# A list schedule of its own for an attention and gated-MLP kernel, and float16 halves for the row of reciprocals

## The chip, the core and the metric

The kernel runs on one NeuronCore of a Trainium2 chip. The core has five engines with one instruction queue each: TensorE (PE: matrix products, with weight loads shown apart as PEld), VectorE (DVE), ScalarE (ACT), GpSimd (POOL) and SyncE (SP, which here only issues DMAs). Each queue is worked off in its order; engines wait for each other by semaphores. The metric is the device time of one execution in microseconds (us), lower is better.

## The reference

Attention over 8 batches, 12 heads, 448 positions, 64 columns, with an RMS norm on queries and keys, and then a gated MLP that mixes positions:

```python
q_n, k_n = (rmsnorm(q, g_q), rmsnorm(k, g_k))          # x / sqrt(mean(x*x) + 1e-6) * g
scores = scale * np.matmul(q_n, k_n.transpose(0, 1, 3, 2))
scores = scores - np.max(scores, axis=-1, keepdims=True)
attn = np.exp(scores)
attn = attn / (np.sum(attn, axis=-1, keepdims=True) + 1e-09)
x = np.matmul(attn, v)                                  # heads side by side: (8, 448, 768)
h = gelu_tanh(x @ w_in)                                 # 768 -> 1024
u, v = h[..., :512], h[..., 512:]
v_n = (v - mean(v)) / np.sqrt(var(v) + 1e-6) * g_ln
v_s = np.einsum('ts,bsd->btd', w_sg, v_n) + b_sg[None, :, None]
out = x + (u * v_s) @ w_out                             # 512 -> 768
```

Everything is float32. The kernel keeps that precision with pairs of float16 numbers: a value is split into a high half and the rest, and a product is made of three (high x high, high x low, low x high).

## The kernel before, in words

The work goes by *head pairs*: two heads of one batch, 48 pairs in all, index `i`; two pairs with the same loads form a unit `u` (24 of them), six pairs a batch `b`.

- For a unit, `load_qk` brings queries and keys; `squares` and `norms` make the reciprocal norms (ScalarE squares, VectorE sums, L311, L312); `split` multiplies them in on GpSimd (L336, L337), makes the float16 halves (L341 ScalarE, L342 GpSimd) and transposes them by DMA into `qt`.
- `scores(u)` has seven tiles `t`. For each tile six (or twelve half-height) matmuls write two banks (L418), VectorE takes the maximum (`nm`, L421), ScalarE the exponential with its sum (`ex`, L424), ScalarE the high half and VectorE the rest (`ahl`, L427, L428), and SyncE issues the transpose into `at_all` (L433). After tiles 3 and 6 `recips` takes the reciprocals of the sums (L385, L386).
- `pv(i)` first spreads the reciprocals over a row by matmuls against an identity (`recip_row`, L398: eight float32 matmuls, four blocks by two heads; ScalarE copies the row, L401), then makes 3 + 18 matmuls of values and attention (L450, L455), multiplies by the row (L457) and splits the result into the halves of `x` (L459, L460).
- `moe(b)` is the MLP of a batch: `mv` (L517, L520: the half of `w_in` that makes `v`), a cluster of Gelu activations between two table loads (`cluster`, L470 to L479), the layer norm, `mu` (L576), Gelu again, `ms` (L604, L611: the mixing of positions), the gating on GpSimd (L615 to L619), `mo` (L642 to L654: `w_out` and the residual).
- `weights()` decodes `w_in`, `w_sg` and `w_out` once, in the first batch (L150 to L156, L197 to L199, L230 to L256).

TensorE's matmuls come in several *tile forms*: 128*128 (the whole array), 64*128 for scores (two row halves), 128*64 for pv, rows and a part of mv (two column halves), 64*64.

PSUM: two score tiles of two banks (`ps_s`), one bank for rows and pv (`ps_v`), three for all of the MLP (`ps_m`).

What sets the order before: the program is written as generators (`scores`, `pv`, `moe`, `weights`) that the loop at the end advances in turn, by ratios (`SC`, `SV`, `M0`, `M1`, `MR`, `ML`, `WR`), with priorities shifted for the MLP (`MOFF`, `GP`). The tile framework's own scheduler, with its timeline simulation (`TILE_KW`), makes the queues from that. The MLP of batch `b` runs beside the attention of the next batch; those of the first and the last batch use another form of `moe` (`early=True`), in which two mv tiles take each pair's `x` as it comes.

Of the kernel before, what the change touches and what calls it, by code (L numbers as in the profile page):

```python
# [23 lines left out]

MOFF, MOFF0, GP = 200, 100, 350

WR, M0, M1, MR, ML = 3, 8, 7, 11, 11

SLOT = (0, 4, 1, 5, 2, 6, 3)

I0, WD = 5, 6

VC, UC = (3,), (0, 1)

SC, SV = 7, 3
# [5 lines left out]
EXP_SET = "natural_log_exp_and_others"  # L41
BACC_KW = dict(dynamic_dma_scratch_size=1024)
TILE_KW = dict(schedule_with_timeline_sim=True)
# [3 lines left out]
def kernel(  # L47
# [14 lines left out]
    nc = tc.nc  # L62
# [18 lines left out]
    FH = DH // 2  # L81

    const = ctx.enter_context(tc.tile_pool(name="const", bufs=1))
    ld = ctx.enter_context(tc.tile_pool(name="ld", bufs=3))
    prep = ctx.enter_context(tc.tile_pool(name="prep", bufs=2))
    att = ctx.enter_context(tc.tile_pool(name="att", bufs=2))
    sml = ctx.enter_context(tc.tile_pool(name="sml", bufs=4))
    xp = ctx.enter_context(tc.tile_pool(name="xp", bufs=1))
    ps_s = ctx.enter_context(tc.tile_pool(name="ps_s", bufs=NS, space=bass.MemoryType.PSUM))
    ps_v = ctx.enter_context(tc.tile_pool(name="ps_v", bufs=NV, space=bass.MemoryType.PSUM))  # L90
    ps_m = ctx.enter_context(tc.tile_pool(name="ps_m", bufs=NM, space=bass.MemoryType.PSUM))
    mlp = None

    V, A, G = nc.vector, nc.scalar, nc.gpsimd
    mm = nc.tensor.matmul
# [3 lines left out]
    G.memset(ones, 1.0)  # L99
    ident = const.tile([P, P], BF16, name="ident")  # L100
    make_identity(nc, ident)
    ident_f = const.tile([P, P], F32, name="ident_f")
    V.tensor_copy(out=ident_f, in_=ident)
    warm = sml.tile([P, 1], F32, name="warm", bufs=1)
    A.preload_act_table_set(EXP_SET)
    A.activation(out=warm, in_=ones[:, 0:1], func=AF.Square)

    SSW = 2 * C7
# [34 lines left out]

    W = {}

    def decode(dst, raw, tmp):
# [6 lines left out]
        hf = raw.bitcast(F32)[:, :, 1]  # L153
        A.activation(out=tmp, in_=hf, func=AF.Square)
        G.tensor_scalar(out=tmp, in0=tmp, scalar1=LEAST_SQ, scalar2=None, op0=ALU.is_ge)
        G.tensor_tensor(out=dst, in0=dst, in1=tmp, op=ALU.mult)  # L156

    def weights():
        nonlocal mlp
        ctx_w = ExitStack()  # L160

        wi = const.tile([P, KT, 2, DF], F16, name="wi")
        wi_f = wi.rearrange("p t x f -> p t (x f)").bitcast(F32)
        ws_h = const.tile([P, CK, S], F16, name="ws_h")
        ws_l = const.tile([P, CK, S], F16, name="ws_l")
        wo_h = const.tile([P, FT, DM], F32R, name="wo_h")
        wo_l = const.tile([P, FT, DM], F32R, name="wo_l")
        gw = const.tile([P, FT], F32, name="gw")
        bb = const.tile([P, S], F32, name="bb")
        part = const.tile([P, 2 * KT], F32, name="wi_part")  # L170
        stage = ctx_w.enter_context(tc.tile_pool(name="stage", bufs=1))
        WC = DF // 2
        raws = {}

        def load_raw(j):
            if j >= 2 * KT:
                return
            raws[j] = stage.tile([P, WC, 2], I32, name="raw", bufs=RAWB)
            nc.sync.dma_start(out=raws[j].rearrange("p a b -> p (a b)"),
                         in_=wi_b[j // 2 * P:(j // 2 + 1) * P, (j % 2) * 2 * WC:(j % 2 + 1) * 2 * WC])  # L180

        with tc.issue_after(first):
            for j in range(RAWB):
                load_raw(j)
        for j in range(2 * KT):
            dst = wi_f[:, j // 2, (j % 2) * WC:(j % 2 + 1) * WC]
            sq = prep.tile([P, 896], F32, name="sqk", tag="t4", bufs=HLB)
            decode(dst, raws.pop(j), sq[:, 0:WC])
            load_raw(j + RAWB)
            sq2 = stage.tile([P, WC], F32, name="sqw", bufs=2)  # L190
            A.activation(out=sq2, in_=dst, func=AF.Square, accum_out=part[:, j:j + 1])
            yield
        wsc, winv = pow2_scale("wi", part, const)
        W["winv"] = winv
        for t in range(KT):
            tmp = stage.tile([P, DF], F32, name="tmp", bufs=2)
# [3 lines left out]
            yield  # L200
        W.update(wi_h=wi[:, :, 0], wi_l=wi[:, :, 1])
        ctx_w.close()

        mlp = ctx.enter_context(tc.tile_pool(name="mlp", bufs=1))
        W.update(ws_h=ws_h, ws_l=ws_l, wo_h=wo_h, wo_l=wo_l, gw=gw, bb=bb)
        yield

        wsr = [mlp.tile([P, S], F32, name="wsr", tag="ug", bufs=5) for c in range(CK)]  # L210
        for s_ in range(C7):
            nc.sync.dma_start(out=wsr[s_ // 2][s_ % 2 * HP:(s_ % 2 + 1) * HP],
                              in_=w_sg.rearrange("(p c) s -> c p s", c=C7)[SLOT[s_]])
# [7 lines left out]
        yield  # L221
        for c in range(CK):
            np_ = P if c < CM else HP
# [3 lines left out]
            for o, n, src in ((0, C4, cols[:, 0:C4]), (HP, CM, cols[:, C4:C7]), (S, 1, cols[:, CM:C4])):  # L227
                oh, ol = (x[0:np_, o - o % P:o - o % P + n * P].rearrange("t (c p) -> t c p", p=P)[:, :, o % P:o % P + HP]
                          if n > 1 else x[0:np_, o:o + HP].unsqueeze(1) for x in (wph, wpl))
# [24 lines left out]
        for s_ in range(C7):  # L254
            V.tensor_copy(out=bb[:, s_ * HP:(s_ + 1) * HP], in_=bs[:, SLOT[s_]])
        W["done"] = True  # L256

# [534 lines left out]
```

## Time and profile before

| what | value |
|---|---|
| median of 3 runs | 1017.5 us (1015.75 to 1020.56) |
| time of the profiled execution | 1013.41 us |
| its span, first to last instruction | 1011.0 us |
| busy PE / DVE / ACT / POOL | 853.6 / 752.4 / 725.5 / 395.7 us |
| mean granted TensorE clock | 0.925 |
| DMA | 155.68 MB, 448001 packets |

The profile is of one execution. A group row reads: line, engine, operation, output<-inputs, shapes, count | busy us, mean ns of one | idle time of the engine just before them, and who ended it. A row of waits: who waited for whom, us in total, times, longest. A timeline row: start, length, engine, line, operation, count of merged instructions. The ends of matmuls are modelled, so a chain of them looks longer than its starts are apart.

### The profile page before, as it was taken

What the parts mean: (1) busy time and instruction counts of PE and PEld (TensorE: products, weight loads), DVE (VectorE), ACT (ScalarE), POOL (GpSimd) and SP (SyncE); (2) the same over time, 40 slices, a digit from 0 to 9 for tenths busy, and PEclk for the clock granted to TensorE, in tenths of its full rate; (3) what the DMA queues carried; (4) which work ended last, traced back from release to release, by engine and by line L of the source; (5) the groups of instructions that cost most, each with busy time, mean ns of one, the idle gap of its engine ahead of it and who ended that gap; (6) DMA issues with size and microseconds to landing.
All of it is one profiled execution on the core that took longest, in us unless ns stands there. A gap on an engine that the chain in (4) does not pass through costs nothing.

```text
span 1011.0 us, 16516 instructions
## 1 busy us (share of the span) xinstructions
PE 853.6 (84%) x5908; PEld 452.4 (45%) x5908; DVE 752.4 (74%) x1191; ACT 725.5 (72%) x1464; POOL 395.7 (39%) x271
## 2 busy tenths in 40 slices
PE   1334567858999899988999899988999999999998
PEld 0112223424634466434744365344744465445546
DVE  5799988998799787788578876787778964784140
ACT  3676798887788967788678875688678874786241
POOL 2477812658553553135512553225512540004021
PEclk9857597978999989999999999989999998999999
DMA  6987778867999679976876676965976674743102
GB/s 164 224 215 167 164 161 201 175 143 164 183 219 203 144 164 211 204 158 132 173 154 152 144 172 149 194 135 135 205 163 151 112 181 101 157 102 84 37 1 63
DMA packets 448001, 155.68 MB, mean 154 GB/s; under 512 B 404336, under 2 KB 441776, under 8 KB 447920
## 3 DMA queue, kind: packets, MB, share of 16 engines
q1 hardware_dynamic: 447344, 154.18, 69.2%
q8 instruction: 46, 0.75, 0.3%
q10 hardware_dynamic: 576, 0.46, 0.2%
q14 instruction: 35, 0.29, 0.1%
HBM read 43.57 MB, written 11.01 MB: 54 GB/s over the span
## 4 chain that ended last, share of the span: by engine, by line
PE 39%; DVE 24%; ACT 14%; issue 9%; DMA 9%; POOL 4%; SPq 2%; ACTq 0%; POOLq 0%; DVEq 0%
DVE ahl L428 6%; DVE nm L421 5%; PE s L418 5%; ACT ex L424 4%; DMA at<-ahl 4%; PE pv L455 4%; PE row L398 2%; ACT ahl L427 2%; DMA qt<-hl 2%; DVE vl L373 1%; DMA raw<-in_moe_w_in_dram 1%; DVE vl L564 1%; PE pv L450 1%; ACT L470 1%; DVE ss L312 1%
## 5 line engine op out<-in xcount | busy, mean ns | idle before, releaser
L424 ACT ACTIVATE ex<-s,nm 128x448 f32<-128x448 f32 x336 | 209.3, 630 | 77.2 <-DVE nm L421 62.6
L428 DVE TENSOR_TENSOR ahl<-ex,ahl 128x896 f16<-128x896 f32 x168 | 216.7, 1293 | 53.5 <-ACT ahl L427 52.7
L418 PE MATMUL s<-qt 64*128 64x448 f16 (+1 forms) x1152 | 157.1, 387 | 75.1 <-ACT ex L424 62.8
L421 DVE TENSOR_REDUCE nm<-s 128x2 f32<-128x896 f32 x168 | 180.9, 1080 | 34.3 <-PE s L418 34.3
L427 ACT ACTIVATE ahl<-ex 128x896 f16<-128x896 f32 x168 | 159.6, 953 | 27.5 <-DMA at<-ahl 25.6
L342 POOL TENSOR_TENSOR hl<-qk,hl 128x896 f16<-128x896 f32 x46 | 95.5, 2080 | 136.4 <-ACT hl L341 123.3
L337 POOL TENSOR_TENSOR qk<-qk,ny 128x896 f32<-128x896 f32 x46 | 86.4, 1899 | 99.5 <-DVE ny L326 74.0
L418 PEld LDWEIGHTS <-qt 64*128 64x128 f16 (+1 forms) x1152 | 48.9, 101 | 149.9 <-issue 101.5
L615 POOL TENSOR_TENSOR gt<-gt,u 128x448 f32<-128x448 f32 x32 | 42.5, 1336 | 132.8 <-ACT u L585 68.3
L455 PE MATMUL pv<-at,vh 128*64 128x448 f16 x576 | 93.6, 375 | 0.0
L336 POOL TENSOR_TENSOR qk<-qk,gg 128x896 f32<-128x896 f32 x23 | 50.8, 2208 | 85.2 <-ACT sqk L311 79.3
L576 PEld LDWEIGHTS <-wi 128*128 128x128 f16 x576 | 55.1, 99 | 62.4 <-issue 16.0
L398 PE MATMUL row<-ident_f,ry 128*64 128x128 f32 (+1 forms) x768 | 62.7, 295 | 18.4 <-DVE x L460 16.0
L424 ACT ACTIVATION_READ_ACCUMULATOR ex<-s,nm 128x1 f32 x336 | 67.6, 201 | 0.0
L398 PEld LDWEIGHTS row<-ident_f,ry 128*64 128x64 f32 (+1 forms) x768 | 45.8, 149 | 44.9 <-issue 36.6
L517 PEld LDWEIGHTS <-x 128*128 128x128 f16 x432 | 37.4, 99 | 59.7 <-issue 18.7
L312 DVE TENSOR_REDUCE ss<-sqk 128x14 f32<-128x896 f32 x48 | 51.7, 1077 | 14.4 <-ACT sqk L311 14.2
L341 ACT ACTIVATE hl<-qk 128x896 f16<-128x896 f32 x48 | 45.5, 949 | 18.3 <-POOL qk L337 13.3
L455 PE MATMUL pv<-at,vl 128*64 128x448 f16 x288 | 54.7, 372 | 0.0
L311 ACT ACTIVATE sqk<-qk 128x896 f32<-128x896 f32 x48 | 45.6, 949 | 12.3 <-DMA qt<-hl 4.8
L455 PEld LDWEIGHTS <-vh 128*64 128x64 f16 x576 | 34.0, 114 | 40.3 <-issue 23.8
L457 DVE TENSOR_TENSOR pv<-pv,row 128x448 f32<-128x448 f32 x48 | 30.0, 625 | 23.1 <-PE pv L455 23.0
(967 smaller groups left out, 1818.4 us busy)
## 6 DMA issues: line engine op xcount, KB each, us to landing
out_dram<-ot SPq DMA_DIRECT2D x56, 192.0 KB, 2.9
vr<-in_v_dram SPq DMA_DIRECT2D x32, 192.0 KB, 3.3
raw<-in_moe_w_in_dram SPq DMA_DIRECT2D x12, 512.0 KB, 5.2
qk<-in_q_dram SPq DMA_DIRECT2D x47, 128.0 KB, 2.9
qk<-in_k_dram SPq DMA_DIRECT2D x47, 128.0 KB, 2.8
vr<-in_v_dram SPq DMA_DIRECT2D x32, 144.0 KB, 3.2
qk<-in_q_dram SPq DMA_DIRECT2D x47, 96.0 KB, 2.6
qk<-in_k_dram SPq DMA_DIRECT2D x47, 96.0 KB, 2.6
```

What stands on the lines that cost most here:

```text
L312: V.tensor_reduce(out=SS[u][:, x], in_=skv, axis=AX.X, op=ALU.add)
L336: E.tensor_tensor(out=qk, in0=qk, in1=gg.unsqueeze(1).broadcast_to([P, SSW, D]), op=ALU.mult)
L337: E.tensor_tensor(out=qk, in0=qk, in1=r["rs"][:, x * SSW:(x + 1) * SSW].unsqueeze(2).broadcast_to([P, SSW, D]), op=ALU.mult)
L342: E.tensor_tensor(out=l_, in0=r["qk"][:, x], in1=h_, op=ALU.subtract)
L398: mm(out=ps[h * HP:(h + 1) * HP, o:o + w], lhsT=y[ks, 2 * n + h:2 * n + h + 1].broadcast_to([w, HP]), rhs=ident_f[ks, ks], start=(n == 0), ...
L418: mm(out=ps[r_, h, 0:S], lhsT=qt[hs, qx, t * P + r_.start:t * P + r_.stop], rhs=qt[hs, kx, j * S:(j + 1) * S], start=(m == 0), stop=(m == 2))
L421: V.tensor_reduce(out=nm, in_=ps[:, :, 0:S], axis=AX.X, op=ALU.max, negate=True)
L424: A.activation(out=ex[:, h], in_=ps[:, h, 0:S], func=AF.Exp, bias=nm[:, h:h + 1], accum_out=sums[:, t, h:h + 1])
L427: A.activation(out=ahl[:, 0], in_=ex, func=AF.Copy)
L428: V.tensor_tensor(out=ahl[:, 1], in0=ex, in1=ahl[:, 0], op=ALU.subtract)
L455: mm(out=ps[h * HP:(h + 1) * HP], lhsT=vx[:, c + h * (C4 + 1)], rhs=at_all[:, n + c + h * C4, o:o + S], start=False, stop=(c == CM - 1 and ...
L576: done = mm(out=ps[:, 0:S], lhsT=ww[:, g, f * P:(f + 1) * P], rhs=xx, start=(n == 0), stop=(n == 17))
```

## The change

All engines' calls now go through recorders. `Engine` turns `V.tensor_tensor(...)` into an entry of `Plan`; `Pool` notes every tile, its tag and its number of buffers. Nothing is issued while the program is written down. `Plan.close` makes an operation of one call or of a `group()` of calls (all matmuls of a scores tile, of a row, of a pv, a cluster of Gelus with its table loads) and finds its predecessors from the regions read and written. Each operation has a `due`: its place in the program (`base`, in head pairs) plus an offset of its kind (`OFF`).

`cost` gives each a duration from formulas; `order` is the list schedule: at each step it takes the engine that can start first, and of that engine's ready operations the one with the smallest due (on TensorE with `sw` added where the tile form differs from the last). It keeps time for semaphores between engines, for buffers that come free, for VectorE and GpSimd excluding each other on operations that read two SBUF tensors, for a change of tile form (95 ns) and for TensorE at half speed after a gap. `emit` then issues everything in that order under a manual schedule.

Beside it: the row of reciprocals is made from float16 halves (`rh`, `rl`) against a float16 identity, 16 matmuls for 8 and two more small VectorE operations per pair; pv is one group that also waits for the copy of its row; `moe` has one form for all batches, its mv tile for the last 64 positions comes first as one group of 36, and mv, mu and ms groups wait for a Gelu cluster (`gate`); the stages of `weights` use the memory of `wo_h` and `wo_l` where a pool of their own was. Transfers, tile shapes, the other matmuls and the numbers of buffers stay.

```diff
-MOFF, MOFF0, GP = 200, 100, 350
-WR, M0, M1, MR, ML = 3, 8, 7, 11, 11
-TILE_KW = dict(schedule_with_timeline_sim=True)
+TILE_KW = dict()
+OFF = dict(
+    load=-2.8823,
+    vload=-2.061,
+    sq=28.9908,
+    ss=-3.3192,
...
+    qt=-16.647,
...
+    s=-0.2793,
+    nm=-0.1353,
+    ex=0.3831,
+    ah=0.2586,
+    al=0.6002,
+    at=-5.206,
+    rec=0.6318,
+    row=-35.3134,
+    rowc=-10.0423,
+    pv=-18.0955,
...
+    w0=-4.4259,
+    w1=0.3245,
...
+    mv=0.9793,
+    mvs=0.1109,
+    gv=10.6048,
...
+    mo=6.1784,
...
+    tail=25.4349,
+    sw=0.1675,
+)
...
+    def cost(self, op, items):
...
+            if name.startswith("dma_start"):
+                if "transpose" in name:
+                    op.dur, op.land, op.gap = (1560.0, 2080.0, 50.0) if self.free(writes[0]) > 700 else (1250.0, 1700.0, 50.0)
+                else:
+                    op.dur, op.land, op.gap = 605.0, 2150.0 if n < 1000 else 3600.0, 50.0
...
+    def cost_pe(self, op, items):
...
+            c = max(106.0, n * 0.95) if dt == F32 else n * (0.33 if n == 256 else 0.4185 if n > 200 else 0.44) + (13.0 if dt == F32R else 0.0)
+            if prev is not None:
+                if ts != prev[0]:
+                    t += prev[1] + 95.0
+                    used = set()
+                elif dt == F32 or ts == (128, 128) or pos in used:
+                    t += prev[1]
+                    used = set()
+                else:
+                    t += 3.0
...
+    def order(self):
...
+                t = min(max(r, f + ops[i].gap) for r, i in rs)
+                if pick is None or t < pick[0]:
+                    pick = (t, e, rs)
...
+            for r, i in rs:
+                if max(r, free[e] + ops[i].gap) <= t:
+                    p = ops[i].due
+                    if e == PE and cfg is not None and ops[i].mms[0] != cfg:
+                        p += sw
+                    if best is None or (p, i) < best:
+                        best = (p, i)
...
+    def emit(self):
+        with self.tc.manual_schedule():
+            for i in self.order():
+                for f in self.ops[i].run:
+                    f()
...
     def recips(i):
...
-        x = sml.tile([P, 2 * C4], F32, name="rx", bufs=2)
-        U[u]["r", j] = y = sml.tile([P, 2 * C4], F32, name="ry", bufs=3)
+        x, y = (sml.tile([P, 2 * C4], F32, name=f"r{c}", bufs=2) for c in "xy")
+        U[u]["r", j] = rh, rl = [sml.tile([P, 2 * C4], F16, name=f"r{c}", bufs=3) for c in "hl"]
         V.tensor_scalar(out=x, in0=sums, scalar1=1e-9, scalar2=None, op0=ALU.add)
         V.reciprocal(out=y, in_=x)
+        V.tensor_copy(out=rh, in_=y)
+        V.tensor_tensor(out=rl, in0=y, in1=rh, op=ALU.subtract)
...
+                for x, rx in enumerate(U[u]["r", j]):
+                    for h in range(2):
+                        mm(out=ps[h * HP:(h + 1) * HP, o:o + w], lhsT=rx[ks, 2 * n + h:2 * n + h + 1].broadcast_to([w, HP]),
+                           rhs=ident_h[ks, ks], start=(n == 0 and x == 0), stop=(n == CM and x == 1), skip_group_check=True)
...
+        with at("pv"), plan.group((done,)):
...
-            if early and t == 1 and g == NP - 1:
-                cluster([gelu_v(i) for i in range(2)], done)
...
+                    for g, (xh, xl) in enumerate(X):
+                        plan.base = b0 + o["mvs"] * (s_ * NP + g)
+                        with plan.group(gate):
...
     for i in range(NI):
...
+        pv(i)
+        if i == NP - 1:
+            weights()
+        if g == NP - 1:
+            moe(b)
+    plan.emit()
```

More of the change, by code (lines that the diff above doesn't have):

```diff
@@ new lines, with __init__, tile @@
+SIZE = {F32: 4, F32R: 4, I32: 4, F16: 2, BF16: 2}
+PE, DVE, ACT, POOL, SP = range(5)
+DMA = 5
+class Op:
+    __slots__ = ("eng", "run", "deps", "tiles", "due", "dur", "gap", "lock", "land", "mms", "last", "kind")
+class Pool:
+    def __init__(self, plan, pool, bufs, name):
+        self.plan, self.pool, self.bufs, self.pname = plan, pool, bufs, name
+    def tile(self, shape, dtype, name, tag=None, bufs=None):
+        n = self.bufs if bufs is None else bufs
+        kw = dict(name=name, bufs=n)
+        if tag is not None:
+            kw["tag"] = tag
+        t = self.pool.tile(shape, dtype, **kw)
+        self.plan.register(t, shape, dtype, (self.pname, tag or name), n, (self.pname, name))
+        return t
@@ L98 @@
+    mlp = pool("mlp", 1)
+    ps_s = pool("ps_s", NS, space=bass.MemoryType.PSUM)
+    ps_v = pool("ps_v", NV, space=bass.MemoryType.PSUM)
+    ps_m = pool("ps_m", NM, space=bass.MemoryType.PSUM)
+    V, A, G, T, Y = (Engine(plan, e, x) for e, x in (
+        (DVE, nc.vector), (ACT, nc.scalar), (POOL, nc.gpsimd), (PE, nc.tensor), (SP, nc.sync)))
+    mm, at = T.matmul, plan.at
+    lo, hi = slice(0, HP), slice(HP, P)
     ones = const.tile([P, P], F32, name="ones")
-    G.memset(ones, 1.0)
     ident = const.tile([P, P], BF16, name="ident")
-    make_identity(nc, ident)
@@ L172, in weights @@
         WC = DF // 2
[L173 to L184, printed above, removed]
         for j in range(2 * KT):
+            plan.base = o["w0"] + o["w1"] * j
@@ new lines, in pv, with cluster @@
+        xh, xl = (x_all[:, i % NX, n] for n in range(2))
+        with at("mul"):
+            V.tensor_tensor(out=ps, in0=ps, in1=row, op=ALU.mult)
+        with at("xh"):
+            A.activation(out=xh, in_=ps, func=AF.Copy)
+        with at("xl"):
+            V.tensor_tensor(out=xl, in0=ps, in1=xh, op=ALU.subtract)
+        XT[i] = (xh, xl)
+    gate = ()
+    def cluster(acts):
+        with plan.group():
+            A.preload_act_table(AF.Gelu_apprx_tanh)
+            for a in acts:
+                a()
+            A.preload_act_table_set(EXP_SET)
@@ L487, in moe @@
+    def moe(b):
+        nonlocal gate
+        o = OFF
+        X = [XT.pop(b * NP + g) for g in range(NP)]
+        last = b == B - 1
+        b0 = NP * (b + 1) + (o["tail"] if last else 0.0)
+        plan.base = b0
         hs = sml.tile([P, 1], F32, name="hs", bufs=2)
@@ L537, in layernorm @@
+        with at("gv", b0 + o["mvs"] * CK * NP):
+            cluster([gelu_v(t) for t in (CM, *range(CM))])
+        plan.base = b0
+        with at("ln"):
+            for t in range(CK):
+                st = sml.tile([P, 6], F32, name="st")
+                V.bn_stats(out=st, in_=vg[:, tiles[t][1]])
+                V.bn_aggr(out=mv[:, t], in_=st)
             sw = ps_m.tile([P, 512], F32, name="sw_", tag="mm")[:, 0:2]
```

918 lines of the change are left out of this document (554 added, 364 removed).

## The prediction

> **What bounds the kernel now.** I read the page first (busy shares, the 40 slices), then the table of stretches, cut where the kernel changes its character, then the waits of the long middle stretch.
>
> ```profile
> span 1011.0 us, 16516 instructions
> PE 853.6 (84%) x5908; PEld 452.4 (45%) x5908; DVE 752.4 (74%) x1191; ACT 725.5 (72%) x1464; POOL 395.7 (39%) x271
> PE   1334567858999899988999899988999999999998
> DVE  5799988998799787788578876787778964784140
> ```
>
> TensorE is thin in the first eight slices, where VectorE is full; from the eleventh on TensorE is full and VectorE is not. So there are two regimes, and the stretches give each its size (columns: length, busy us with instruction count for PE, PEld, DVE, ACT, POOL, then granted clock, DMA share, GB/s):
>
> ```profile
> core 0: us, PE busy (x) PEld busy (x) DVE busy (x) ACT busy (x) POOL busy (x), PEclk, DMA share, GB/s
> 0.00:20.00 20.00, 1.59 (x12) 1.12 (x12) 9.46 (x15) 7.53 (x10) 1.91 (x13) 1.00 0.56 153
> 20.00:267.00 247.00, 152.63 (x1017) 75.84 (x1017) 220.29 (x337) 187.32 (x381) 141.49 (x88) 0.79 0.78 180
> 267.00:846.00 579.00, 541.19 (x3804) 286.15 (x3802) 449.24 (x698) 442.01 (x905) 230.77 (x147) 0.96 0.77 165
> 846.00:937.00 91.00, 89.26 (x665) 45.76 (x665) 60.99 (x107) 65.12 (x133) 11.49 (x13) 1.00 0.52 116
> 937.00:1011.00 74.00, 68.90 (x416) 43.57 (x414) 12.38 (x36) 23.55 (x37) 10.05 (x12) 0.99 0.13 33
> ```
>
> A (20 to 267, weights decoded beside the first head pairs): VectorE 220 of 247 us, 89%: it is the bound. B (267 to 846): TensorE 541 of 579 us, 93%, VectorE 78%, ScalarE 76%, DMA 77%. C and D (846 to 1011): TensorE 158 of 165 us, VectorE 73; C is full with the backlog of batch 6's MLP, D is batch 7's MLP alone. So outside A the time is TensorE's ledger, and a change pays only by what it takes from that ledger, until VectorE, ScalarE and DMA at some 77% become the next bound.
>
> What the 541 us hold is not all streaming. In B, PE idles 38 us, and a clock of 0.96 costs up to 0.04 x 579 = 23 us. Who makes it wait:
>
> ```profile
> ACT ex L424 <- DVE nm L421: 48.9, 36, 5.3
> PE row L398 <- DVE x L460: 11.8, 7, 3.7
> PE s L418 <- ACT ex L424: 10.5, 7, 3.8
> ```
>
> These are waits of the softmax ring (scores, maximum, exponential, split, transpose): single waits up to 3.8 us at TensorE's head, so a matter of order, not of one slow engine.
>
> **Tile forms.** TensorE's timeline at one place of B:
>
> ```profile
> 505.45 0.63 PE L520 MATMUL mv__5264<-wi,x 128*64 128x256 f16 x8
> 506.01 0.39 PE L517 MATMUL mv__5314<-wi,x 128*128 128x512 f16 x1
> 506.33 0.30 PE L520 MATMUL mv__5264<-wi,x 128*64 128x256 f16 x1
> 506.56 0.39 PE L517 MATMUL mv__5314<-wi,x 128*128 128x512 f16 x1
> ...
> 511.03 1.04 PE L517 MATMUL mv__5314<-wi,x 128*128 128x512 f16 x4
> 511.90 0.38 PE L517 MATMUL mv__5337<-wi,x 128*128 128x512 f16 x1
> ```
>
> Alone between two others, one 512-wide and one 256-wide matmul take 506.56 - 506.01 = 0.55 us. In runs they take (511.90 - 511.03)/4 = 0.22 and (506.01 - 505.45)/8 = 0.07. So two changes of form cost 0.26, one 0.13 us. Going through the PE rows of B one by one, from the first to the last of these, the form changes 559 times:
>
> ```profile
> 267.08 0.64 PE L358 MATMUL psv<-vr 128*128 128x128 bf16 x8
> ...
> 845.96 0.32 PE L646 MATMUL mo__8766<-idn,xt 128*64 128x128 bf16 x1
> ```
>
> That is 73 us of B. It is the largest thing that an order alone can lower.
>
> **The change, step by step.**
>
> *Grouped matmuls and a price on a form change.* The new plan moves whole groups (6 for a scores tile, all 21 of pv, all 16 of a row, 3 or 6 of mv and mu, 12 of ms) and adds a penalty to a group of another form. How many changes stay? B holds 112 score tiles, which is 32 head pairs:
>
> ```profile
> 267.00:846.00 579.00, 145.75 (x112) 105.72 (x111) 0.96 0.77 165
> ```
>
> (the stretch row of ahl, its VectorE and ScalarE instructions). Per pair 3.5 score groups alone among others make 7 changes, pv and row some 3 each: 13 x 32 = 416, and some 60 of the five MLPs: 476 at worst, -83 x 0.13 = -11 us. Where half of the score groups come in twos, 350: -27. I take 420: **-18 us**.
>
> *Row halves in float16.* A row is now eight float32 matmuls, each shown as two records:
>
> ```profile
> 514.87 1.14 PE L398 MATMUL row<-ident_f,ry 128*64 128x128 f32 x16
> 515.94 0.39 PE L517 MATMUL mv__5337<-wi,x 128*128 128x512 f16 x1
> ...
> 935.92 0.51 PE L642 MATMUL mo__9803<-idn,x 128*128 128x128 bf16 x6
> 936.24 0.42 PE L654 MATMUL mo__9803<-wo_h,gh 128*128 128x384 f32 x1
> ...
> L385 DVE TENSOR_SCALAR rx<-sums 128x8 f32<-128x8 f32 x48 | 17.4, 363 | 20.0 <-ACT ex L424 19.3
> L386 DVE RECIPROCAL ry<-rx 128x8 f32<-128x8 f32 x48 | 9.5, 198 | 0.9
> ```
>
> It holds TensorE 515.94 - 514.87 = 1.07 us. After, 16 float16 matmuls of 64 columns, in eight pairs on the two column halves. The nearest row, the six of L642, takes (936.24 - 935.92)/6 = 0.053 each. If the halves run side by side: 8 x 0.053 = 0.43, with 0.17 for the change of form 0.6. If they follow one another: 16 x 0.053 + 0.17 = 1.02. So a row saves 0.05 to 0.47; I take 0.3, since every 64-column pair of pv in this kernel starts within some ns of its partner: 0.3 x 32 = **-10 us** in B (bounds -1 to -15). The Trainium skill, "TensorE: Matmul & The Clock Gate", section Back-to-back issue gap, speaks against it: a sustained stream of weight load and matmul at 128 columns takes about 81 ns each; by that a row is 16 x 0.081 = 1.3 us, an estimate, and the term would be +7 instead of -10. The 0.053 of L642 does not bear the 81 ns out. On VectorE the two new small operations (copy and difference of eight columns) cost 0.2 to 0.36 each, 0.4 to 0.7 per pair, 13 to 23 us over B's 32 pairs; they lie in VectorE's 130 idle us of B, and would count in full only if VectorE became the bound.
>
> *The new order itself.* One list schedule with durations near the trace's (1080 ns for the 896-wide maximum, the same 3.6 us from issue to landing of a transpose) replaces the streams and their ratios. It adds and removes no other work on the long lines; what it can take is PE's 38 idle us and the 23 us of low clock that follow them, 61 in all. No row shows the new order. Best: it takes 50 of these. Worst: a pinned order that meets late landings adds 15. I take half, **-30 us**, since the waits above are many and short, and order is what they hang on. B: -18 - 10 - 30 = -58 (bounds -92 to +3).
>
> *A.* Its bound is VectorE, so nothing of the above counts; order counts only by lock-outs against GpSimd:
>
> ```profile
> L428 DVE TENSOR_TENSOR ahl<-ex,ahl 128x896 f16<-128x896 f32 x168 | 216.7, 1293 | 53.5 <-ACT ahl L427 52.7
> L421 DVE TENSOR_REDUCE nm<-s 128x2 f32<-128x896 f32 x168 | 180.9, 1080 | 34.3 <-PE s L418 34.3
> L342 POOL TENSOR_TENSOR hl<-qk,hl 128x896 f16<-128x896 f32 x46 | 95.5, 2080 | 136.4 <-ACT hl L341 123.3
> ```
>
> The split (two SBUF inputs) takes 213 ns longer than the maximum over equally many columns, 36 us over the kernel, 39 x 0.213 = 8 in A. With those and some of A's 27 idle us: **-10**, bounds -22 to +8 (the new row operations of 11 pairs uncovered).
>
> *C and D.* Six rows (-2) and fewer form changes (-3). The form of the MLP for the first and last batch, which advances two mv tiles before the last head pair is done, goes, and with it two pairs of table loads. The chain of waits shows that it bought little at the end: mv of batch 7 starts after the last matmul of batch 6:
>
> ```profile
> 941.82 2.08 PE mo__9898 L654 x12
> 943.90 2.39 PE mv__9958 L517 x11
> ```
>
> If it did count, two tiles x 18 matmuls x 0.22 = +8. I take **-5** (bounds -15 to +8).
>
> **Sum.** -10 - 58 - 5 = -73 us on the profiled execution's own 1013.4 us (span 1011.0 and 2.4 around it): 940. That execution lies 4 us under the median of the runs, 1017.5, so for a median: **944 us**. All bounds together: -129 to +19.
>
> **Rivals.**
> 1. *Dense like A everywhere.* TensorE ceases to be the bound, and VectorE runs at the 89% that A shows. Its work ahead of D is 9 + 220 + 449 + 61 = 740, plus 19 for the new row operations, less the 36 of lock-outs: 723. (723 - 9)/0.89 + 20 + 74 = 896 us of span, **903** as a median. For it: B leaves 130 us of VectorE idle. Against: ScalarE and DMA would both have to pass from 77% to near 90% too.
> 2. *Only the countable part.* Waits and clock stay, since they come from PSUM and SBUF buffers whose numbers do not change: -18 - 10 - 5 = -33: **984**. For it: VectorE and ScalarE wait on each other in one ring, 48.9 us above.
> 3. *Slower, by late transposes.* All queues are pinned for fixed landings; the pv group now is one block that waits also for the copy of its row, and everything behind it on TensorE waits with it.
>
> ```profile
> L433 SPq DMA_TRANSPOSE at<-ahl x176: 1228/1492/4472, 38.3 to 924.1; - x176
> DMA to landing us min/median/max: 3.1/3.7/7.7
> ```
>
> If one transpose in three (59) lands 2 us later than planned and holds TensorE, that is +118 - 73 = +45: **1062**. It decides from 37 such landings on. Against it: the order of before is fixed on the chip as well, and TensorE's own waits on transposes are not among the large ones above.
> 4. *No change*: the gains and such stalls cancel, 1017.
>
> **How the numbers follow.** Forecast 944 (its own range 925 to 965): 0.44; the first rival 0.27; the second 0.16; the slower one 0.09; no change 0.04. The range 890 to 1005 holds the first three but for their edges. About 0.5% (5 us) is what a measurement of this kernel can tell from no change: faster 0.87, the same 0.04, slower 0.09.
>
> **What would show it.** Right, if in the profile after TensorE's form changes in the middle fall to some 400, a row holds it about 0.75 us, granted clock there is 0.98 or more, and a head pair takes some 16 us there instead of 18. The first rival shows as VectorE over 85% through the middle with TensorE idle between groups; the second as the same ACT ex waits and clock with fewer form changes; the third as PE waits on transposes of tens of us and the weight load of pv among them. I would be wrong at the root if the end comes late because the last batch's MLP stands alone for much longer than D's 74 us.

## The result, and the profile after

After: 1005.64 us median of 4 runs (1002.82 to 1007.62); before: 1016.62 median of 4 (1015.48 to 1020.56). The ratio is 0.9883, with a 95% interval of 0.9845 to 0.9921: faster by 1.2%. The sign of the forecast holds; its 944 us don't, and the time lies just above the range. All times below are medians; ratios are to the kernel before as measured beside each run (1014.6 to 1016.6).

The page of the kernel after, whose operations all have the helper's line L194 (first lines, the slices of TensorE and VectorE, and the head of the chain of waits), then the table of its stretches (columns as in that of before), cut at the same places except that the last batch's MLP begins at 929:

```profile
span 1005.8 us, 16559 instructions
...
PE 782.6 (78%) x5908; PEld 430.1 (43%) x5908; DVE 781.7 (78%) x1287; ACT 724.5 (72%) x1463; POOL 393.9 (39%) x271
...
PE   1304364688789798987998879888897899998988
...
DVE  6798899969788889879887988699887986775120
...
PE 27%; DVE 21%; ACT 20%; DMA 16%; issue 8%; SPq 4%; POOL 4%; ACTq 0%; POOLq 0%; DVEq 0%
DMA at<-ahl 12%; PE pv L194 7%; ACT ex L194 5%; DVE ahl L194 5%; ACT ahl L194 4%; SPq L194 4%; DVE nm L194 4%; PE s L194 3%; DMA qk<-in_k_dram 2%; ACT L194 2%; DVE wi L194 2%; DVE vl L194 2%; ACT vh L194 1%; PE row L194 1%; POOL gl L194 1%
```

```profile
0.00:20.00 20.00, 1.60 (x12) 1.13 (x12) 12.12 (x21) 6.27 (x10) 1.89 (x12) 1.00 0.79 220
20.00:267.00 247.00, 128.51 (x878) 57.59 (x882) 213.82 (x338) 178.86 (x360) 127.73 (x76) 0.82 0.72 164
267.00:846.00 579.00, 509.40 (x4033) 285.55 (x4035) 487.28 (x794) 460.80 (x945) 242.00 (x160) 0.98 0.83 171
846.00:929.00 83.00, 75.62 (x574) 39.70 (x575) 55.99 (x100) 56.78 (x115) 12.42 (x12) 0.96 0.52 111
929.00:1006.00 77.00, 67.47 (x418) 46.17 (x417) 12.48 (x36) 21.83 (x36) 9.90 (x12) 0.95 0.12 31
```

TensorE was relieved: 853.6 us of busy time have become 782.6. The span of the profiled execution fell by 5 us. In the middle, TensorE's busy time fell by 32 us and its idle time rose by the same 32, from 38 to 579 - 509.4 = 69.6, with more instructions done there; VectorE went from 449 to 487. The chain of waits of before read:

```profile
PE 39%; DVE 24%; ACT 14%; issue 9%; DMA 9%; POOL 4%; SPq 2%; ACTq 0%; POOLq 0%; DVEq 0%
DVE ahl L428 6%; DVE nm L421 5%; PE s L418 5%; ACT ex L424 4%; DMA at<-ahl 4%; PE pv L455 4%; PE row L398 2%; ACT ahl L427 2%; DMA qt<-hl 2%; DVE vl L373 1%; DMA raw<-in_moe_w_in_dram 1%; DVE vl L564 1%; PE pv L450 1%; ACT L470 1%; DVE ss L312 1%
```

TensorE's share of it went from 39 to 27%, that of the landing transposes (`at<-ahl`) from 4 to 12%. The waits of before, then of after, over the whole span:

```profile
PE s L418 <- ACT ex L424: 62.8, 24, 11.4
ACT ex L424 <- DVE nm L421: 62.6, 47, 5.3
...
ACT ahl L427 <- DMA at<-ahl: 25.6, 27, 2.3
```

```profile
PE s L194 <- ACT ex L194: 82.2, 49, 8.0
ACT ahl L194 <- DMA at<-ahl: 62.5, 57, 4.1
...
PE pv L194 <- DMA at<-ahl: 18.6, 16, 2.8
PEld L194 <- DMA at<-ahl: 16.7, 12, 3.3
```

ScalarE now waits 62.5 us for transposes to give back the buffer of the attention halves; TensorE's pv and its weight loads wait for them too.

Where the 5 us of span are: the multiplications by the row (48 in all, one per pair) show the progress. The ninth and the forty-second, of before and then of after:

```profile
246.08 0.62 DVE L457 TENSOR_TENSOR pv<-pv,row 128x448 f32<-128x448 f32 x1
...
834.61 0.63 DVE L457 TENSOR_TENSOR pv<-pv,row 128x448 f32<-128x448 f32 x1 [3.53 <-PE pv L455]
```

```profile
252.59 0.62 DVE L194 TENSOR_TENSOR pv<-pv,row 128x448 f32<-128x448 f32 x1
...
827.77 0.63 DVE L194 TENSOR_TENSOR pv<-pv,row 128x448 f32<-128x448 f32 x1 [1.02 <-PE pv L194]
```

Up to the ninth +6.5, between them 588.5 to 575.2 = -13.3, behind them 176.4 to 178.0 = +1.6. The middle's 33 pairs went from 17.8 to 17.4 us each, where 16 were forecast.

### The profile page after: what moved, and what is told of

Same layout as the page of the kernel before. It is cut to its first block, busy times and chain, and to the rows that moved or that the text cites. A ratio compares the mean times of both kernels' runs of the same rounds, so it can differ in the third digit from the quotient of the medians.

```text
span 1005.8 us, 16559 instructions
## 1 busy us (share of the span) xinstructions
PE 782.6 (78%) x5908; PEld 430.1 (43%) x5908; DVE 781.7 (78%) x1287; ACT 724.5 (72%) x1463; POOL 393.9 (39%) x271
## 4 chain that ended last, share of the span: by engine, by line
PE 27%; DVE 21%; ACT 20%; DMA 16%; issue 8%; SPq 4%; POOL 4%; ACTq 0%; POOLq 0%; DVEq 0%
DMA at<-ahl 12%; PE pv L194 7%; ACT ex L194 5%; DVE ahl L194 5%; ACT ahl L194 4%; SPq L194 4%; DVE nm L194 4%; PE s L194 3%; DMA qk<-in_k_dram 2%; ACT L194 2%; DVE wi L194 2%; DVE vl L194 2%; ACT vh L194 1%; PE row L194 1%; POOL gl L194 1%
## 5 line engine op out<-in xcount | busy, mean ns | idle before, releaser
L194 DVE TENSOR_TENSOR ahl<-ex,ahl 128x896 f16<-128x896 f32 x168 | 220.3, 1313 | 60.2 <-ACT ahl L194 59.4
L194 ACT ACTIVATE ex<-s,nm 128x448 f32<-128x448 f32 x336 | 209.2, 627 | 45.8 <-DVE ahl L194 22.5
L194 ACT ACTIVATE ahl<-ex 128x896 f16<-128x896 f32 x168 | 159.1, 947 | 64.2 <-DMA at<-ahl 62.5
L194 PE MATMUL s<-qt 64*128 64x448 f16 (+1 forms) x1152 | 134.6, 381 | 86.8 <-ACT ex L194 82.2
L194 DVE TENSOR_REDUCE nm<-s 128x2 f32<-128x896 f32 x168 | 179.8, 1082 | 15.5 <-PE s L194 15.1
L194 PE MATMUL pv<-at,vh 128*64 128x448 f16 (+1 forms) x672 | 131.5, 393 | 34.8 <-DMA at<-ahl 18.6
L194 POOL TENSOR_TENSOR qk<-qk,ny 128x896 f32<-128x896 f32 x46 | 88.0, 1931 | 160.5 <-DVE ny L194 154.3
L194 PEld LDWEIGHTS <-vh 128*64 128x64 f16 (+2 forms) x928 | 65.7, 112 | 123.2 <-issue 72.0
L194 POOL TENSOR_TENSOR hl<-qk,hl 128x896 f16<-128x896 f32 x46 | 93.9, 2048 | 49.8 <-ACT hl L194 48.5
L194 PEld LDWEIGHTS <-qt 64*128 64x128 f16 (+1 forms) x1152 | 46.8, 101 | 155.4 <-issue 119.1
L194 POOL TENSOR_TENSOR qk<-qk,gg 128x896 f32<-128x896 f32 x23 | 51.2, 2227 | 150.4 <-ACT sqk L194 125.6
L194 PEld LDWEIGHTS <-x 128*128 128x128 f16 (+1 forms) x1056 | 75.1, 104 | 69.5 <-issue 29.0
L194 POOL TENSOR_TENSOR gt<-gt,u 128x448 f32<-128x448 f32 x32 | 39.1, 1241 | 158.6 <-DVE gt L194 158.5
L194 PEld LDWEIGHTS <-wi 128*128 128x128 f16 x576 | 55.4, 100 | 64.8 <-issue 12.1
L194 PE MATMUL pv<-at,vl 128*64 128x448 f16 (+1 forms) x336 | 75.3, 390 | 0.0
L194 PE MATMUL row<-ident_h,rh 128*64 128x128 f16 (+1 forms) x384 | 35.3, 235 | 46.3 <-DVE rh L194 45.8
L194 ACT ACTIVATION_READ_ACCUMULATOR ex<-s,nm 128x1 f32 x336 | 66.8, 199 | 0.0
L194 DVE TENSOR_TENSOR pv<-pv,row 128x448 f32<-128x448 f32 x48 | 30.1, 628 | 35.0 <-PE pv L194 34.9
L194 ACT ACTIVATE sqk<-qk 128x896 f32<-128x896 f32 x48 | 45.2, 944 | 15.4 <-DMA qk<-in_q_dram 8.8
L194 DVE TENSOR_REDUCE ss<-sqk 128x14 f32<-128x896 f32 x48 | 51.6, 1078 | 5.0 <-ACT sqk L194 4.8
L194 ACT ACTIVATE hl<-qk 128x896 f16<-128x896 f32 x48 | 45.2, 942 | 8.2 <-POOL qk L194 7.5
L194 PEld LDWEIGHTS <-rh 128*64 128x64 f16 (+1 forms) x384 | 21.2, 113 | 68.9 <-DVE rh L194 55.3
```

The costliest lines, as they stand in the source:

```text
L194: item = (eng, name, lambda: f(*args, **kw), reads, writes, kw)
```

## The experiments

### Is the time TensorE's ledger?

**e1: before, with a third of mu left out.**

```diff
                 for xx, ww in ((xh, wi_h), (xl, wi_h), (xh, wi_l)):
-                    done = mm(..., start=(n == 0), stop=(n == 17))
+                    if n % 3 != 2:
+                        done = mm(..., start=(n == 0), stop=(n == 16))
```

> The kernel before without the third product (high half of x by low half of w_in) of mu: 192 matmuls of 0.189 us are left out, 36 us of TensorE and nothing of any other engine; the scheduler of before orders what is left. Theory of the prediction (TensorE's ledger is the time outside the first 267 us): 25 to 36 us less than before. Rival (the ring of scores, maximum, exponential, split and transpose sets the pace, TensorE only fills it): 0 to 10 us less, most of it in the last batch, which stands alone (4.5 us).

1030.01 us, ratio 1.0142 [1.0099, 1.0186]: slower, with less work, and outside both expectations. In the middle TensorE is busy 510.73 us where it was 541.19, and the time went up. But the scheduler of before makes other queues from the changed program: of the 1190 pairs of neighbours in VectorE's queue of before, 563 are still neighbours. So this run doesn't settle it.

**e2: after, the same work left out, its order held fixed** (the plan's order of all 3872 operations written into the kernel):

```diff
-                        mm(out=ps[:, 0:S], ..., start=(n == 0), stop=(n == 17))
+                        mm(out=ps[:, 0:S], ..., start=(n == 0), stop=(n == 16), leave=n % 3 == 2)
```

> The changed kernel with every instruction in the changed kernel's own order, but the third product of mu left out (192 matmuls, 36 us of TensorE). Ledger theory: 25 to 36 us less than the changed kernel (970 to 980). Ring theory: 4 to 10 us less (about 998), because TensorE already idles 70 of 579 us in the middle and the last batch alone gives 4.5.

1005.31 us, 0.9899 [0.9853, 0.9944]. TensorE's busy time is 756.9 instead of 782.6 us; the time is that of after. Neither expectation holds: not even the 4 us of the last batch came. The middle of e2, then that of e6 below (columns as above):

```profile
267.00:846.00 579.00, 496.88 (x3940) 275.97 (x3936) 483.09 (x798) 462.83 (x948) 243.44 (x161) 0.96 0.80 173
```

```profile
267.00:846.00 579.00, 523.59 (x4044) 296.29 (x4040) 466.44 (x729) 460.84 (x948) 243.44 (x161) 0.97 0.82 171
```

The granted clock in the middle is 0.96 in e2 against 0.98 in after, which takes back part of the relief; what stays of it changes nothing. In the order of after, TensorE is not what sets the time.

**e5 and e6: the rows.** e5 gives the kernel before float16 rows and nothing else; e6 gives the kernel after its float32 rows back, in its fixed order, without the two VectorE operations.

```diff
 # e5 (before)
+        V.tensor_copy(out=rh, in_=y)
+        V.tensor_tensor(out=rl, in0=y, in1=rh, op=ALU.subtract)
-                   rhs=ident_f[ks, ks], start=(n == 0), stop=(n == CM)
+                       rhs=ident_h[ks, ks], start=(n == 0 and x == 0), stop=(n == CM and x == 1)
 # e6 (after): these lines the other way round
```

> One part of the change alone: the kernel before with the row of reciprocals made from float16 halves (16 matmuls of half the time for 8, two more small VectorE operations per head pair), ordered by the scheduler of before. Ledger theory: 0.3 to 0.45 us of TensorE less per pair, 14 to 22 us less than before. Rival (TensorE is not what sets the time, and every new order that the scheduler makes scatters by some us): within 8 us of before, with either sign.

> One part undone: the changed kernel in its own order with the float32 row of before (8 matmuls; the two small VectorE operations per pair are gone). Ledger theory: 0.43 us more of TensorE per pair, 15 to 21 us more than the changed kernel (1020 to 1027). Theory of missed durations (the order was laid for durations that the chip does not keep; VectorE's chains of dependent small operations and SyncE's transposes are what runs late): the two operations that go stand in such a chain, so 0 to 8 us less than the changed kernel (998 to 1006).

e5: 1033.33 us, 1.0185 [1.0139, 1.0230], slower and outside both expectations. e6: 1005.13 us, 0.9906 [0.9876, 0.9936], as after and as the theory of missed durations has it, though TensorE has 523.6 us of work in the middle against 509.4; VectorE has 25 us less over the span (756.7 for 781.7), which changes nothing either. In e1 and e5 a small relief ends 14 and 18 us later; what these two share is that the old scheduler planned anew (in e5 367 of the 1190 pairs remain). That the new order is the reason isn't shown by a run.

### Is it the ring's buffer?

e3 and e4 leave out a little work to make room in SBUF, alike in both; e4 then has three `ahl` buffers instead of two. Both in the fixed order.

```diff
 # e3, e4
-            gth, gtl = (mlp.tile([P, FT, P], F32R, name=f"gt{c}") for c in "hl")
+            gth = gtl = mlp.tile([P, FT, P], F32R, name="gth")
 # e4 alone: the pool holds one more than the plan counts
-  name="ahl", bufs=NAH)
+  name="ahl", bufs=NAH, real=NAH + 1)
```

> Control for the next one: the changed kernel in its own order; left out are the low half of the gated values and the copied residual in the output tile that two batches share (32 small GpSimd operations, 4 copies, 32 matmuls); the memory this frees is not used. All theories: 0 to 8 us less than the changed kernel, 998 to 1006.

> The same as the control, in the same order, but with three buffers instead of two for the split attention weights (ahl), so that ScalarE's split waits for the transpose of three tiles ago and not of two. Only this wait is relaxed. Ring theory: a buffer is held 8.6 us on average from the split to the landing of its transpose, two of them give a pace of at least 4.3 us a tile against 4.96 measured, so the third takes away most of ScalarE's 62 us of waiting for transposes: 25 to 50 us less than the control. Theory of missed durations (the plan's late sum comes mostly from chains of small dependent VectorE operations and from SyncE's issue, only some 15 to 19 us of it from late landings at the ahl buffers): 10 to 20 less. Ledger theory: within 3 us of the control.

1002.75 (0.9895 [0.9839, 0.9951]) and 1002.06 us (0.9877 [0.9829, 0.9924]): no difference. So e4 misses what was expected from the buffer (25 to 50 us less) and from the missed durations (10 to 20 less); the ledger's expectation, which it fits, falls with e2 and e6. The waits of e3, then those of e4, where ScalarE's wait for transposes has no row any more:

```profile
ACT ahl L360 <- DMA at<-ahl: 60.4, 56, 4.1
...
DVE pv L360 <- PE pv L360: 30.2, 19, 7.1
```

```profile
DVE pv L360 <- PE pv L360: 61.6, 28, 6.6
...
PEld L360 <- DMA at<-ahl: 21.1, 13, 3.3
```

The wait at the buffer was where the lateness showed, not where it came from: VectorE waits longer for TensorE's pv instead, and TensorE's weight loads still wait for the landings.

### What are the loads worth?

e7 (after, fixed order) and e8 (before) leave out the loads of queries, keys and values once the first buffers are filled; e12 is e7 with thin loads instead.

```diff
 # e7                                          # q, k; the same for v
-    Y.dma_start(out=qk[...], in_=src[...])
+    Y.dma_start(out=qk[...], in_=src[...], leave=u >= NQK)
 # e12
+    # THIN = 16 columns of each row once u >= NQK
+    Y.dma_start(out=qk[...][:, :, 0:THIN], in_=src[...][:, :, c0 * D:c0 * D + THIN])
```

> The changed kernel in its own order without the loads of q and k after the first two units and of v after the first six head pairs (the arithmetic runs on what was loaded first; some 400 loads and 31 MB of the 155 are left out). What stays on the DMA queues are the transposes and the output. Theory of missed durations: transposes then take what the plan gives them (1.56 us of issue and 2.1 to land, against 1.69 and 2.38 on average now), and the time falls by 10 to 38 us, to 967 to 995. If the DMA side is hidden anyway: within 5 us of the changed kernel, 1000 to 1008.

> The kernel before with the same loads left out, ordered by its own scheduler. If late transposes and loads cost the kernel before as much as the changed one: 10 to 38 us less than before. If it has the slack for them (its buffers of split weights are held 7.2 us of 2 x 5.2 available, against 8.6 of 2 x 5.0 after): within 8 us of before.

> The kernel after in its own fixed order; the loads of queries and keys after the first two units, and those of values after the first six pairs, are issued as before but bring 16 columns of each row in place of all (64 B of 768 or 1024 B), so later units work on old data. Nearly all of the bytes go, the number of issues and of rows stays. If the 28 us that came back without loads were due to the bytes in the way of the transposes: 977 us, 970 to 985. If they were due to SyncE's time for issuing loads, or to the number of rows: 1000 to 1006.

e7: 977.27 us, 0.9629 [0.9584, 0.9674], 28 us less than after (26 by the ratios); what it leaves out are 232 loads and 30 MB. e8: 1018.28, 1.0031 [1.0009, 1.0053], no gain. e12: 991.56, 0.9767 [0.9719, 0.9815], half of e7's. So these loads cost the order of after 28 us. About half goes with the bytes; the other half with the issues on SyncE or the number of rows, which no run separates. e12 lies between its two expectations: neither alone holds. In e7 the transposes `at` came part of the way to the plan, with means of 1.62 us to issue and 2.22 from there to landing, against 1.69 and 2.38 in after and 1.56 and 2.08 in the plan. What the loads cost the order of before e8 doesn't show: its scheduler planned anew (270 of the 1190 pairs remain), and e1 and e5, planned anew as well, lost 14 and 18 us, which could hide a gain of that size. ScalarE's wait for transposes in after, e7 and e12:

```profile
ACT ahl L194 <- DMA at<-ahl: 62.5, 57, 4.1
```

```profile
ACT ahl L360 <- DMA at<-ahl: 32.9, 31, 2.5
```

```profile
ACT ahl L361 <- DMA at<-ahl: 37.3, 38, 2.7
```

### Are the plan's durations what is missing?

The kernel's own list schedule, worked through without a chip, ends at 921.8 us; the chip's span is 1005.8. Set beside the trace, operation by operation, the chip's first `nm` starts 4 us later than planned, the 25th 24, the 73rd 54, the last 93: lateness grows all along. Two durations of the plan differ from the trace. First, it starts every VectorE operation 81 ns before the end of the one ahead (ScalarE 102, GpSimd 42), also where it needs that one's result. VectorE's timeline of after:

```profile
509.32 1.07 DVE L194 TENSOR_TENSOR ahl<-ex,ahl 128x896 f16<-128x896 f32 x1
510.32 0.28 DVE L194 TENSOR_TENSOR vpart<-psv,ident 128x128 f32<-128x128 f32 x1
...
511.60 0.18 DVE L194 TENSOR_TENSOR nt<-nx,ny 128x28 f32<-128x28 f32 x1
511.81 0.19 DVE L194 TENSOR_TENSOR nt<-nt,ny 128x28 f32<-128x28 f32 x1
...
515.09 0.15 DVE L194 TENSOR_SCALAR v_x<-v_x 128x1 f32<-128x1 f32 x1
515.28 0.15 DVE L194 TENSOR_SCALAR v_i<-v_x 128x1 int32<-128x1 int32 x1
```

`vpart` needs nothing of `ahl` and starts at 510.32, 70 ns before that ends at 510.39. `nt` needs the `nt` before it and starts 30 ns after its end (511.78); `v_i` 40 ns after `v_x`. The medians over all such places of the trace: VectorE -82 where independent and +34 where dependent (415 places), ScalarE -93 and +122 (75), GpSimd +84. ScalarE's +122 is read too high. Most of its places are a split behind an exponential, and between the two stands the read of the exponential's sum, which the plan's duration of the exponential already holds:

```profile
345.98 0.62 ACT L194 ACTIVATE ex<-s,nm 128x448 f32<-128x448 f32 x1
346.49 0.20 ACT L194 ACTIVATION_READ_ACCUMULATOR ex<-s,nm 128x1 f32 x1
346.72 0.95 ACT L194 ACTIVATE ahl<-ex 128x896 f16<-128x896 f32 x1
```

The exponential ends at 346.60 and the read at 346.69; the split starts at 346.72, 120 ns behind the one and 30 behind the other. Counted from the last instruction ahead, ScalarE's median is +32, much like VectorE's. The corrected plans below use 122, some 90 ns too long behind an exponential.

Second, transposes: planned at 1.56 us to issue and 2.08 from there to landing; in the trace the means are 1.69 and 2.38 for `at`, 1.79 and 2.32 for `qt`, with one in eight (30 of 224) over 3 us to landing.

To weigh them I replayed the order of after: each operation starts when its engine's queue, its inputs and its buffers are ready. With the plan's durations it ends at 921.8, with dependent gaps 954.5, with the transposes' and loads' own times alone 971.3, with both 995.2, with every measured duration 1009.4. With VectorE's dependent gaps alone it ends at 948.5, and with all three but 32 in place of 122 for ScalarE at 951.8: VectorE carries this term. This is arithmetic. The runs test it: new orders from plans with corrected durations, chosen by a search over `OFF` that is judged by the plan's own end, or by the replay with transposes and loads scattered as in the trace.

```diff
 # "gaps" (e9, e11, e14, e15)
+    DEP = (0.0, 34.0, 122.0, 84.0)
-                v = fin[i] + l if ops[u].eng != e or o.land >= 0 else free[e] + ops[u].gap
+                v = fin[i] + (l if ops[u].eng != e or o.land >= 0 else self.DEP[e] if 0 < e < 4 else ops[u].gap - 165.0 * (e == 0))
 # "transfers" (e9, e11, e14, e16)
-    op.dur, op.land, op.gap = (1560.0, 2080.0, 50.0) if ...
+    op.dur, op.land, op.gap = (1700.0, 2370.0, 50.0) if ...
-    op.dur, op.land, op.gap = 605.0, 2150.0 if n < 1000 else 3600.0, 50.0
+    op.dur, op.land, op.gap = 605.0, 2600.0 if n < 1000 else 3600.0, 50.0
 # e9, e10, e13 to e16: new values in OFF (46 offsets)
```

> The kernel after, planned anew with three durations put right from its own trace: a vector, scalar or GpSimd operation that needs the result of the one right before it on its engine starts 34, 122 or 84 ns after that one's end (and not before it), a transpose takes 1.70 us to issue and 2.37 us from there to land (1.56 and 2.08 before), a load 2.6 us (2.15). With them the offsets of the dues were searched for anew. What is computed stays. Worked out by replaying the fixed order with transposes and loads that scatter as in the trace, this order ends at 968.5 us where the order of after ends at 995.3; after takes 1005.6 on the chip, 10 us more. Missed durations: 979 us, 975 to 990. Rival, that a planner's length says little about the chip because what slows the chip is not in any of these numbers: 1000 to 1015, as after.

> Control for the run with corrected durations: the kernel after with its own durations unchanged, and the same kind of search for other offsets. Its plan ends at 916.7 us instead of 921.8. By the replay with dependent gaps and scattered transposes 990.7 (after: 995.3). Missed durations: about 1001 us, 994 to 1008, hardly other than after. If instead any new search helped: under 990.

> The three corrected durations alone, with the offsets of after, so that the order changes but nothing was searched for. Its plan ends at 980.2 us, its replay at 1011.4, against 995.3 for after. Missed durations as a replay weighs them: 1022 us, 1010 to 1030, slower than after although the durations are nearer the chip's; better durations help only through the search that they allow. Rival, that right durations are worth something by themselves at each choice of the schedule: under 1000.

> The run of 971 us had two things that the control of 999 us had not: corrected durations in the plan, and a search that judged each order by the replay with scattered transposes instead of by the plan's own end. This kernel has the second alone: the durations of after in the plan, its offsets searched with the replay as judge. Replay 986.9 us; the four planned orders measured so far came out 10, 8, 3 and -3 us from their replays. If the durations that the plan works with are what matters: 985 to 997 us. If the judge of the search is what matters: 970 to 980.

> The other half of the same question: the three corrected durations in the plan, offsets searched with the plan's own end as judge (951.6 us), no replay. Replay 977.6. If the durations matter: 975 to 988 us, faster than the search with the plan's old durations and the replay as judge. If the judge matters: 990 to 1005, as the control.

> One of the two missed durations alone: in the plan an operation that needs the result right before it on its engine starts 34, 122 or 84 ns after that one's end; transposes and loads as in after. Offsets searched with the replay as judge. Replay 986.0 us. If these gaps were the whole of what the plan missed: 970 to 978, as with all corrections. If both durations are needed: 983 to 996.

> The other missed duration alone: transposes 1.70 us to issue and 2.37 to land, loads 2.6 us, dependent operations as in after. Offsets searched with the replay as judge. Replay 989.5 us. If transposes were the whole of what the plan missed: 970 to 978. If both are needed: 985 to 1000.

| run | put right in the plan | searched by | plan's end | replay | median us | ratio |
|---|---|---|---|---|---|---|
| after | - | - | 921.8 | 995.3 | 1005.64 | 0.9883 [0.9845, 0.9921] |
| e10 | - | plan's end | 916.7 | 990.7 | 998.54 | 0.9837 [0.9807, 0.9867] |
| e13 | - | replay | 919.1 | 986.9 | 992.99 | 0.9781 [0.9731, 0.9831] |
| e11 | gaps, transfers | - | 980.2 | 1011.4 | 1008.87 | 0.9951 [0.9929, 0.9972] |
| e14 | gaps, transfers | plan's end | 951.6 | 977.6 | 979.56 | 0.9660 [0.9613, 0.9707] |
| e9 | gaps, transfers | replay | 935.5 | 968.5 | 971.35 | 0.9580 [0.9539, 0.9621] |
| e15 | gaps | replay | 947.5 | 986.0 | 982.40 | 0.9667 [0.9611, 0.9722] |
| e16 | transfers | replay | 937.2 | 989.5 | 991.47 | 0.9763 [0.9710, 0.9817] |

The plan's own end ranks these orders badly: the shortest plans (e10, e13, after) are three of the four slowest on the chip. The replay comes within 11 us each time. With the same judge, corrected durations are worth 999 to 980 (e10, e14) or 993 to 971 us (e13, e9); with the same durations, the other judge is worth 6 to 8. Either correction alone does less than both (982, 991, 971): the gaps alone gain 11 us on e13, the transfers alone 1.5, which isn't clear of the noise. By themselves, without a search for offsets that fit, the corrections gain nothing (e11). Each row stands for one search; how far another one would scatter wasn't measured, so differences of a few us between searched orders are not to be leaned on. e9 came out 4 us under the range given for it, e11 and e15 1 us under theirs. e9 is the fastest of all: 4.2% under before. Its page (span, busy time, chain by engine) and one row of its waits:

```profile
span 968.5 us, 16551 instructions
...
PE 784.7 (81%) x5908; PEld 431.6 (45%) x5908; DVE 755.7 (78%) x1287; ACT 719.3 (74%) x1463; POOL 398.7 (41%) x271
...
PE 39%; ACT 21%; DVE 18%; DMA 10%; issue 6%; POOL 3%; SPq 2%; ACTq 0%; DVEq 0%; POOLq 0%
```

```profile
ACT ahl L194 <- DMA at<-ahl: 46.2, 41, 4.7
```

The work on TensorE is that of after; DMA's share of the chain fell from 16 to 10%, and the last `nm` starts 45 us behind the plan instead of 93.

## Why the prediction was wrong, and where it was right

**The step that failed** is "outside A the time is TensorE's ledger, and a change pays only by what it takes from that ledger", and with it the sum's largest term, -30 for waits and clock. I read 93% busy in the middle as a bound, so that every us taken from TensorE would shorten the time. Of the four signs that I named three came, on TensorE (353 form changes, a row in 0.64 us, a clock of 0.98), and the fourth, the time of a head pair, did not: the 32 us that TensorE gave up in the middle turned into 32 us of waiting. In the order of after, e2 takes 192 matmuls out and changes nothing; e6 puts 14 us back and changes nothing. So an engine that is busy 88% there (509 of 579 us) follows others. For the order of before, with its 93%, no run holds the order fixed, and whether TensorE bounded it stays open. What the runs show in the ledger's place is the plan: gaps between dependent operations and transfer times that it didn't have. With them put right and the offsets searched anew, the same work takes 971 us (e9). The Trainium skill, "Perfetto Trace Analysis", section Identifying the Most-Contended Engine, says that matmul busy time is no good measure of headroom, because matmuls are pipelined, and names weight-load busy time, beside the share of peak arithmetic, instead. Weight-load busy time was 45% before and 43% after; e2 and e6 agree as far as TensorE not being the limit in the order of after.

**Form changes: -18, by 420.** The mechanism held and went further. Counted as before, from the first to the last of these rows, the form changes 353 times instead of 559:

```profile
266.92 1.27 PE L194 MATMUL s<-qt 64*64 64x448 f16 x12
...
845.64 0.66 PE L194 MATMUL pv<-at,vh 128*128 128x448 f16 x3
```

That is 206 x 0.13 = 27 us off TensorE; e2 and e6 say what time off TensorE is worth in this order.

**Rows: -10, by 0.75 us each.** A row of after, and the group behind it:

```profile
509.14 0.22 PE L194 MATMUL row<-ident_h,rh 64*64 64x64 f16 x2
...
509.62 0.22 PE L194 MATMUL row<-ident_h,rl 128*64 128x128 f16 x2
509.78 0.76 PE L194 MATMUL s<-qt 64*64 64x448 f16 x12
```

It holds TensorE 509.78 - 509.14 = 0.64 us: the column halves do run side by side, and 16 matmuls take 0.040 us each, not the 0.081 that I had weighed from the Trainium skill, "TensorE: Matmul & The Clock Gate", section Back-to-back issue gap. The 0.17 that I put on the change of form stands on no row (one change had come to 0.13), and the 1.3 us by 0.081 leaves that change out; that 0.6 lies so near 0.64 is partly luck. Off TensorE again, worth nothing by e6. The two VectorE operations are 0.17 us each in the median, as priced.

**Waits and low clock: -30.** Here the size and the sign were off. The clock of the middle came to 0.98 as hoped. But the waits didn't shrink: they grew by 32 us, with 6% more matmuls done in the same 579 us (4033 for 3804). I halved TensorE's idle time because its waits were "many and short, and order is what they hang on". Order it was; but this order is laid for a chip on which a dependent operation starts at once and a transpose lands on time, and I had noted that its durations are "near the trace's" without asking after the gaps between operations. Long VectorE and ScalarE operations are within some 1% of the trace in the median; the gaps and transfers were off. For transposes I compared medians; their mean in before was 1.66 us to issue and 2.28 to landing, together 0.3 above the plan's 3.64.

**A: -10; C and D: -5.** Up to the ninth pair 6.5 us were lost, where A was to gain 10, and no run tells why; behind the forty-second 1.6 were lost. The last batch's MLP ran from 943.9 to 1011.0 before, 67.1 us, and from 936.1 to 1005.8 after, 69.7. The 2.6 us more may be what the early form was worth or go with the granted clock (0.99 before, 0.95 after in the last stretch); no run separates them.

**The rivals.** The first (VectorE at 89%) did not come: 487 of 579 us are 84%, and e6 takes VectorE work out without gain. The second has the likeness (gains that don't reach the end) but put the cause in buffers. For the buffers of the attention halves e4 refutes that: waits shifted, the time stayed. The others, PSUM's among them, were not varied, but e9 gains over 30 us on after with all numbers of buffers as they were. The third has a part of the mechanism: late transposes in a pinned order, pv among those that wait. I priced it as 59 landings of 2 us on top of a full gain. What came is gentler, a steady lateness that cost most of the gain and not more, and by e15 and e16, one search each, more of it lies with the dependent gaps, which no rival named. The third's test, PE waits of tens of us on transposes with pv's weight load among them, is met: 18.6 and 16.7.

What stays open: how e7's 28 us divide between SyncE's issues and the number of rows, what the loads cost the order of before, and what a plan with ScalarE's gap at 32 would give.

## What to carry to other kernels

A high busy share of an engine whose queue is fixed is no bound until taking work off that engine has moved the time; try that, with the order held fixed, before adding up savings. A planner that plans anew from a changed program mixes the change with another order, as in e1, e5 and e8. A kernel that carries its own schedule is as good as its model of what lies between operations: set the plan beside the trace operation by operation and look at where lateness grows. This plan, with its long operations right to 1%, ended 84 us before the chip did. And judge a plan by replaying it with scattered transfers rather than by its own end.

## What the runs showed of the hardware

On VectorE an operation that needs the result right before it starts 116 ns later, against that one's profiled end, than one that doesn't (-82 to +34); on ScalarE 125 (-93 to +32, counted from the end of the read of the sum where one stands between). The Trainium skill, "Perfetto Trace Analysis", section Optimizing Scalar/DVE Operations, says that the profiled latency is about twice an instruction's data-access overhead (on SBUF some 60 ns for VectorE, 93 for ScalarE), since the write-acknowledgement half overlaps with the next instruction. The -93 of independent successors on ScalarE agrees with that; VectorE's -82 is more than 60.

A small VectorE operation can be held as long as a GpSimd operation beside it runs: the copy of eight columns into `rh` takes 171 ns in the median, and up to 1.86 us. In that longest case GpSimd had started a difference of two tensors 60 ns ahead (the first of the two in its row):

```profile
L194 DVE CAST rh<-ry x48: 141/171/1861, 77.9 to 919.1; 128x8 f16<-128x8 f32 x48
```

```profile
503.70 4.67 POOL L194 TENSOR_TENSOR hl<-qk,hl 128x896 f16<-128x896 f32 x2
503.76 1.86 DVE L194 CAST rh<-ry 128x8 f16<-128x8 f32 x1
```

Five of the 48 copies take over 0.4 us; each overlaps a GpSimd operation, four of them one with two input tensors, and ends 24 to 28 ns before that one does.

Transposes between SBUF tiles get a little slower when loads are under way: with them the median from issue to landing is 3.8 us in after, without them 3.6 in the same order (e7). The longest took 6.5 us with them and 8.3 without, so the tail isn't the loads' alone.
